# Attention and two expert layers on one core: the queue that issues the transfers of Pool's and VectorE's results

## The chip, the core and the metric

The kernel runs on one core of a Trainium2 chip. The metric is the device time of one execution in microseconds (us), the median of three runs. The engines are TensorE (PE in the profile, its weight loads PEld), VectorE (DVE), ScalarE (ACT), Pool (GpSimd) and SyncE (SP), which here only issues transfers. A transfer is issued by an instruction on an engine's queue and carried out by 16 DMA engines. Transfers that SyncE issues are those of queue q1 in the profile (hardware_dynamic), transfers that Pool issues are those of q0 (software_dynamic).

## What is computed

Three stages follow one another. Only the first is touched by the change. Cut to what matters:

```python
def _attn_ref(q, k, v):                       # (4, 8, 768, 64): batch, heads, positions, width
    block, window = (32, 16); nb = S // block # 24 blocks
    k_sum = k.reshape(B, H, nb, block, D).max(axis=3)
    v_sum = v.reshape(B, H, nb, block, D).mean(axis=3)
    # each position sees its neighbours within 15 places, and the 24 block summaries
    ...
    return np.matmul(a, np.concatenate([v, v_sum], axis=2))
...
x = attn_out.transpose(0, 2, 1, 3).reshape(B * S, H * D)   # 3072 rows of 512
x = _moe_ref(x=x, **moe_kwargs)       # one of 8 experts per row, or none
return _moe2_ref(x=x, **moe2_kwargs)  # 8 experts with 384 rows each, chosen greedily
```

## The kernel before

The attention is `phase_a`. Its work is cut into eight units (a batch and four of its heads), numbered 0 to 7, and each unit into six steps, so that a loop runs over 48 steps and a few more. A step makes four products of queries and keys on TensorE (`qk`, line 128), masks them on VectorE (line 132), takes exponentials on ScalarE, transposes the result, and multiplies it by the values (`pv`, line 154, two steps behind `qk`; the first steps wait until step 4). VectorE divides by the sums (lines 156 to 162). Two units make a batch. After every batch VectorE works out the gate of the first expert layer (`gate1` to `gate3`) and the rows of the batch go to a table in DRAM, `xrows` (line 202), which the first expert layer gathers from.

What a unit needs is loaded by `load`: keys `kt` (line 78) and queries `qd` (line 79) in two halves each, the values once as blocks in `vn` (line 81, the tile is called wraw in the profile), and once in the order in which the products need them, in `VV` (line 85, two transfers into partitions 24 to 119). Partitions 0 to 23 of `VV` take the 24 block means. Those are made by `prep_v`: Pool adds up `vn` in halves (line 118), divides by 32 (line 120), and four transfers, one for each head, copy the 24 rows of means to the twelve places in `VV` (line 122). So a unit's `VV` is complete only when line 85 and line 122 have both landed, and `pv` of the unit's first step waits for that.

`load(u+2)` is written into the second step of unit u. It issues the keys and queries of unit u+2, then calls `prep_v(u+1)`, and then issues the values of unit u+2. For unit 1 the first halving is on VectorE (line 116). The order of the instructions on each engine is the order of the code (the schedule is written by hand), and each queue issues in its order: an instruction that waits holds up everything behind it on its queue. Buffers: `kt` has three, `qd` two, `VV` three, and the raw tiles four. VectorE takes the maxima of the keys in `prep_k` (line 101) and copies them with `prep_kc` (lines 108 and 109).

Of the kernel before, what the change touches and what calls it, by code (L numbers as in the profile page):

```python
# [45 lines left out]
def phase_a(nc,tc,ctx,I,st):  # L46
# [15 lines left out]
    for i in range(2):  # L62
        t=cp.tile([128,2,12,128],F32,name=f"Q2_{i}"); Q2.append(t)
        for h in range(2):
            (G if i else V).memset(t[0:64,h,:,64:128],0.0); G.memset(t[64:128,h,:,0:64],0.0)
    for i in range(3):
        t=cp.tile([24+VP,12,4,65],F32,name=f"VV_{i}")
# [6 lines left out]
    def load(u):  # L74
        b,g=units[u]
        kt=ld.tile([128,2,KW],F32,name="kt",bufs=3); qd=ld.tile([128,2,S],F32,name="qd"); vn=st["raw"].tile([128,2048],F32,name="wraw")[0:96]
        vv=VV[u%3]; src=I['v65']
        def ld_k(h0,h1): nc.sync.dma_start(kt[:,h0:h1],I['k'][b,:,2*g+h0:2*g+h1,:])
        def ld_q(h0,h1): nc.sync.dma_start(qd[:,h0:h1],I['q'][b,:,2*g+h0:2*g+h1,:])
        def ld_v():  # L80
            nc.sync.dma_start(vn,I['v'][b,4*g:4*g+4].rearrange("h (n k) d -> (h n) (k d)",k=32))
        def ld_vv():
            for (s0,s1) in ((0,6),(6,12)):
                ap=bass.AP(tensor=src.tensor,offset=src.offset+(b*2+g)*VR*260+64*260*s0,ap=[[260,VP],[64*260,s1-s0],[1,260]])
                nc.sync.dma_start(vv[24:24+VP,s0:s1].rearrange("p s h d -> p s (h d)"),ap)
        U[u]=dict(kt=kt,qd=qd,vn=vn,vv=vv,q2=Q2[u%2],k2=K2[u%2])
        U[u]['ks']=wk.tile([128,2,24],F32,name="ks",bufs=2)
        ld_k(0,1); ld_q(0,1)
        if u==0: nc.sync.dma_start(cst,I['cst'])
        if u==2: yield; prep_v(1,V)  # L90
        ld_k(1,2); ld_q(1,2)
        if u==0: ld_v(); ld_vv(); nc.sync.dma_start(w17,I['w17'])
        if u==1: prep_v(0,G)
        if u>2: prep_v(u-1,G)
        if u: ld_v(); ld_vv()
        yield
# [16 lines left out]
    def prep_v(u,eng):  # L113
        d=U[u]; vn,vv=d['vn'],d['vv']
        vs2=wk.tile([96,64],F32,name="vs2",bufs=2); w=1024
        if eng is V: V.tensor_reduce(vs2,vn[:,w:2*w].rearrange("p (k d)->p d k",d=64),AX.X,OP.add); w//=2
        while w>=64:
            G.tensor_tensor(vn[:,0:w],vn[:,0:w],vn[:,w:2*w],op=OP.add); w//=2  # L118
        if eng is V: G.tensor_tensor(vn[:,0:64],vn[:,0:64],vs2,op=OP.add)
        G.tensor_scalar(vs2,vn[:,0:64],1.0/32,None,op0=OP.mult)  # L120
        for h in range(4):
            nc.sync.dma_start(vv[0:24,:,h,0:64],vs2[24*h:24*h+24,None,:].to_broadcast([24,12,64]))
    X={}; XT={}; D={}
    def qk(i):
        u,pairs=steps[i]; d=U[u]
# [59 lines left out]
    def group(b,t):  # L185
        return (3,b*NT) if b==B-1 and t==2 else (6,b*NT) if b<B-1 and t==5 else None
# [9 lines left out]
    def gate2(b,t):  # L196
        if group(b,t):
            n,c=group(b,t); c0=c-b*NT; x=X[b][:,c0:c0+n,:]; d,r=D['gd',c]
            s=wk.tile([128,6],F32,name="g_s",bufs=2)[:,0:n]; V.tensor_reduce(s,d,AX.X,OP.add)
            V.tensor_scalar(s,s,1e-9,None,op0=OP.add)  # L200
            V.reciprocal(x[:,:,512],s)
            nc.sync.dma_start(st['xrows'][128+128*c:128+128*(c+n),:].rearrange("(t p) d -> p t d",p=128),x)
            next(r)
    def gate3(b,t):
        if group(b,t): next(D['gd',group(b,t)[1]][1],None)
    def stages(b,t):

        if b<B-2: return tuple(zip(STAGES,(gate1,gate2,gate3,gate3,gate3)))
        if b==B-2: return tuple(zip(STAGES3,(gate1,gate2,gate3,first1,gate3,gate3,first2,first3)))
        return ((1,gate1),(2,gate2),(3,gate3),(4,gate3),(4,gate3))  # L210
# [14 lines left out]
    n=len(steps)  # L225
# [3 lines left out]
    for i in range(n+PL+3):  # L229
        u,t=(i//NT,i%NT)  # L230
# [897 lines left out]
```

## Time and profile before

| | |
|---|---|
| time before, median of 3 runs | 684.64 us (684.58 to 686.84) |
| the profiled execution's own time | 682.42 us |
| its span | 680.8 us |
| busy share of the span: PE, DVE, ACT, POOL | 89%, 75%, 46%, 53% |
| q1 (issued by SyncE): packets, MB | 49968, 79.37 |
| q0 (issued by Pool): packets, MB | 9744, 34.02 |

The span runs from the first to the last instruction of the profiled execution, and its own time is a little more. Busy shares are means over stages with different limits, so a change in one stage has to be read from that stage: the attention takes about the first 176 us. In rows of a timeline the number ahead is the start in us from the beginning of the span, the second the length; in brackets stands how long the engine was idle before, and who ended that.

### The profile page before, as it was taken

The page shows a single profiled execution, that of the slowest core. Times are in us where ns is not written, and L with a number is a line of the kernel's source. Part 1 is how long each engine was busy: PE and PEld are TensorE (multiplying, and loading weights), DVE is VectorE, ACT ScalarE, POOL GpSimd, SP SyncE. Part 2 cuts the span into 40 slices and gives each one's busy share as a digit, 9 for nine tenths or more (in the row PEclk, how much of TensorE's full clock was granted, in tenths as well). Part 3 has the DMA queues.
Part 4 walks back from the last instruction along what each step waited for, and adds up shares of the span by engine and source line. Part 5 has one row for each costly group of instructions (what it writes and reads, how often), then busy time and mean ns, then how long its engine had stood idle before and what let it go on. Part 6 is the DMA issues. An engine that isn't in the chain of part 4 may idle for free.

```text
span 680.8 us, 12765 instructions
## 1 busy us (share of the span) xinstructions
PE 604.4 (89%) x4424; PEld 494.0 (73%) x4427; DVE 508.0 (75%) x1896; ACT 314.2 (46%) x672; POOL 359.0 (53%) x388
## 2 busy tenths in 40 slices
PE   8769896899788999989447999999999999999996
PEld 5658775778466776666226778888797978879895
DVE  5788985999896899994675778788888888862120
ACT  6557774787235676461014235162533426154521
POOL 5234323535462463761016359494876939399841
PEclk9889997999689999898559999999999999999999
DMA  9999999969309968610026063453626254385201
GB/s 258 256 241 249 241 234 206 281 115 339 136 16 324 294 207 287 204 62 23 2 87 208 2 227 115 166 175 124 202 76 203 79 187 155 139 258 180 105 1 46
DMA packets 59778, 114.22 MB, mean 168 GB/s; under 512 B 13537, under 2 KB 23521, under 8 KB 58944
## 3 DMA queue, kind: packets, MB, share of 16 engines
q1 hardware_dynamic: 49968, 79.37, 40.6%
q0 software_dynamic: 9744, 34.02, 15.1%
q8 instruction: 35, 0.57, 0.4%
q14 instruction: 31, 0.25, 0.1%
HBM read 96.54 MB, written 14.88 MB: 164 GB/s over the span
## 4 chain that ended last, share of the span: by engine, by line
PE 18%; issue 11%; POOL 11%; DVE 6%; DMA 3%; ACT 1%; POOLq 1%; DVEq 0%
POOL wl L932 9%; PE dh_ps L961 3%; PE dh_ps L962 3%; PE dh_ps L963 3%; DMA xg<-xrows,p_ix 2%; PE dz_ps L975 2%; PE dz_ps L976 2%; PE dz_ps L977 2%; POOL out_dram L982 2%; DMA wraw<-in_w1b_dram 1%; DVE p_g L793 1%; PE rt_ps L806 1%; PE dx_ps L895 1%; PE dh_ps L950 1%; ACT wh L923 1%
## 5 line engine op out<-in xcount | busy, mean ns | idle before, releaser
L932 POOL TENSOR_TENSOR wl<-wraw,wh 128x512 fp32r<-128x512 f32 x124 | 155.4, 1297 | 5.9 <-ACT wh L923 5.5
L961 PE MATMUL dh_ps<-dxh,wh 128*128 128x384 f32 x256 | 89.2, 349 | 0.7 <-ACT dxh L953 0.7
L923 ACT CAST wh<-wraw 128x512 fp32r<-128x512 f32 x128 | 73.7, 620 | 33.8 <-DMA wraw<-in_w1b_dram 33.4
L962 PE MATMUL dh_ps<-dxl,wh 128*128 128x384 f32 x256 | 86.3, 337 | 0.5 <-DVE dxl L953 0.5
L963 PE MATMUL dh_ps<-dxh,wl 128*128 128x384 f32 x256 | 86.1, 336 | 0.0
L118 POOL TENSOR_TENSOR wraw<-wraw 96x512 f32<-96x512 f32 (+4 forms) x39 | 39.9, 1023 | 80.2 <-DMA wraw<-in_v_dram 77.8
L975 PE MATMUL dz_ps<-wh,dhh 128*128 128x512 f32 x192 | 79.0, 411 | 0.0
L977 PE MATMUL dz_ps<-wh,dhl 128*128 128x512 f32 x192 | 76.0, 396 | 0.0
L976 PE MATMUL dz_ps<-wl,dhh 128*128 128x512 f32 x192 | 75.9, 395 | 0.0
L968 DVE SCALAR_TENSOR_TENSOR dhl<-dh_ps,dhh 128x384 fp32r<-128x384 f32 x64 | 35.1, 554 | 49.0 <-ACT dhh L966 48.7
L982 POOL DMA_INDIRECT out_dram<-dz,io x24 | 24.5, 1023 | 79.5 <-ACT dz L980 76.8
L966 ACT ACTIVATE dhh<-dh_ps 128x384 fp32r<-128x384 f32 x64 | 31.5, 492 | 75.7 <-PE dh_ps L963 74.8
L505 POOL TENSOR_TENSOR wl<-wraw,wh 128x512 fp32r<-128x512 f32 (+1 forms) x26 | 47.8, 1861 | 26.2 <-ACT wh L504 22.7
L980 ACT COPY dz<-dz_ps 128x512 f32<-128x512 f32 x24 | 14.1, 587 | 102.8 <-PE dz_ps L977 56.8
L138 ACT ACTIVATE p_e<-s_sb,nm 128x118 f32<-128x118 f32 x192 | 59.7, 385 | 1.1 <-DVE nm L132 1.1
L128 PE MATMUL s_ps<-kt,Q 128*128 128x118 f32 x192 | 41.4, 299 | 11.6 <-DVE kt L108 9.1
L939 POOL DMA_INDIRECT xg<-xrows,p_ix x24 | 23.3, 972 | 50.9 <-DVE rrow L871 31.3
L961 PEld LDWEIGHTS dh_ps<-dxh,wh 128*128 128x128 f32 x256 | 48.4, 189 | 1.5 <-ACT dxh L953 0.9
L962 PEld LDWEIGHTS dh_ps<-dxl,wh 128*128 128x128 f32 x256 | 48.2, 188 | 1.3 <-DVE dxl L953 1.1
L963 PEld LDWEIGHTS dh_ps<-dxh,wl 128*128 128x128 f32 x256 | 48.1, 188 | 0.0
L504 ACT CAST wh<-wraw 128x1024 fp32r<-128x1024 f32 (+1 forms) x48 | 44.2, 983 | 7.3 <-DMA wraw<-in_w1a_dram 7.1
L132 DVE CUSTOM_DVE_ANT_0 s_sb<-s_ps,cst 128x118 f32<-128x118 f32 x192 | 42.0, 275 | 5.3 <-PE s_ps L128 3.5
(359 smaller groups left out, 1466.5 us busy)
## 6 DMA issues: line engine op xcount, KB each, us to landing
wraw<-in_w1b_dram SPq DMA_DIRECT2D x15, 1024.0 KB
wraw<-in_w2b_dram POOLq DMA_DIRECT2D x14, 1024.0 KB, 7.5
wraw<-in_w2a_dram SPq DMA_DIRECT2D x12, 1024.0 KB
wraw<-in_w1a_dram SPq DMA_DIRECT2D x10, 1024.0 KB
VV<-in_v_dram SPq DMA_DIRECT2D x16, 585.0 KB
kt<-in_k_dram SPq DMA_DIRECT2D x16, 412.0 KB
qd<-in_q_dram SPq DMA_DIRECT2D x16, 384.0 KB
wraw<-in_v_dram SPq DMA_DIRECT2D x8, 768.0 KB
```

The source lines that it names most:

```text
L132: V.tensor_tensor_reduce(out=sb[:,j,:],in0=p[:,j,0:118],in1=mk,scale=-0.125,scalar=3e38,op0=OP.add,op1=OP.min,accum_out=nm[:,j:j+1])
L138: A.activation(pe[:,j,:],sb[:,j,:],AF.Exp,bias=nm[:,j:j+1],scale=-1.0)
L504: (hi.tensor_copy if hi else nc.scalar.copy)(h[:,c],t[:,c])
L505: (lo or nc.vector).tensor_tensor(l[:,c],t[:,c],h[:,c].bitcast(F32),op=OP.subtract)
L923: A.copy(h[:,c],t[:,c])
L932: eng.tensor_tensor(l[:,c],t[:,c],h[:,c].bitcast(F32),op=OP.subtract)
L961: T.matmul(q,wh[:,c],s['xh'][:,d,:],start=(d==0),stop=False)
L962: T.matmul(q,wh[:,c],s['xl'][:,d,:],start=False,stop=False)
L963: T.matmul(q,wl[:,c],s['xh'][:,d,:],start=False,stop=(d==3))
L975: T.matmul(q,s['hh'][:,f,c0],wh[:,c],start=(f==0),stop=False)
L976: T.matmul(q,s['hh'][:,f,c0],wl[:,c],start=False,stop=False)
L977: T.matmul(q,s['hl'][:,f,c0],wh[:,c],start=False,stop=(f==7))
```

## The change

Two lines name another engine for issuing. The four transfers of line 122 and the one of line 202 are issued by Pool in place of SyncE. What they move is the same.

```diff
         G.tensor_scalar(vs2,vn[:,0:64],1.0/32,None,op0=OP.mult)
         for h in range(4):
-            nc.sync.dma_start(vv[0:24,:,h,0:64],vs2[24*h:24*h+24,None,:].to_broadcast([24,12,64]))
+            G.dma_start(vv[0:24,:,h,0:64],vs2[24*h:24*h+24,None,:].to_broadcast([24,12,64]))
...
             V.reciprocal(x[:,:,512],s)
-            nc.sync.dma_start(st['xrows'][128+128*c:128+128*(c+n),:].rearrange("(t p) d -> p t d",p=128),x)
+            G.dma_start(st['xrows'][128+128*c:128+128*(c+n),:].rearrange("(t p) d -> p t d",p=128),x)
             next(r)
```

On SyncE's queue in units 0 and 1 the order changes as follows (kt are keys, qd queries, wraw and VV the values, vs the means).

```order
 L79 DMA qd<-in_q_dram 128x768
-L122 DMA VV_124<-vs_176 24x12x64 x4
 L81 DMA wraw<-in_v_dram 96x2048
 L85 DMA VV_126<-in_v_dram 96x6x260 x2
 L78 DMA kt<-in_k_dram 128x824
 L79 DMA qd<-in_q_dram 128x768
-L122 DMA VV_126<-vs_391 24x12x64 x4
 L78 DMA kt<-in_k_dram 128x824
```

The loads of units 1 and 2 no longer stand behind the means of units 0 and 1.

On the same queue, around unit 4, the piece reads as follows.

```order
-L122 DMA VV_124<-vs_872 24x12x64 x4
 L81 DMA wraw<-in_v_dram 96x2048
 L85 DMA VV_126<-in_v_dram 96x6x260 x2
-L202 DMA xrows<-X_334 128x6x516
 L78 DMA kt<-in_k_dram 128x824
 L79 DMA qd<-in_q_dram 128x768
 L78 DMA kt<-in_k_dram 128x824
 L79 DMA qd<-in_q_dram 128x768
-L122 DMA VV_126<-vs_1174 24x12x64 x4
 L81 DMA wraw<-in_v_dram 96x2048
```

The means of units 3 and 4 and the rows of the first batch have left the queue, and the loads of units 4, 5 and 6 follow each other directly.

On Pool the same transfers have been put in, here behind the sums of unit 3.

```order
 L118 TENSOR_TENSOR wraw<-wraw 96x64
 L120 TENSOR_SCALAR vs_872<-wraw 96x64
+L122 DMA VV_124<-vs_872 24x12x64 x4
 L160 MEMSET X_922 128x6x4
+L202 DMA xrows<-X_334 128x6x516
 L118 TENSOR_TENSOR wraw<-wraw 96x1024
 L118 TENSOR_TENSOR wraw<-wraw 96x512
```

Pool issues the means right behind the multiplication that makes them. The sums of the next unit now stand behind line 202, which waits for VectorE's gate of the first batch.

## Rows read from the trace of the kernel before

**Rows 1.** The page: span, and the share of the DMA engines in 40 slices.

```profile
span 680.8 us, 12765 instructions
...
DMA  9999999969309968610026063453626254385201
```

**Rows 2.** Who waited for whom, VectorE, 0 to 176 us (total, times, longest).

```profile
DVE ks L101 <- DMA kt<-in_k_dram: 11.5, 5, 6.3
```

**Rows 3.** Timeline of VectorE: start, length, what, idle before it and its releaser.

```profile
39.13 0.95 DVE L101 TENSOR_REDUCE ks<-kt 128x24 f32<-128x768 f32 x1 [1.36 <-DMA kt<-in_k_dram]
...
99.13 0.16 DVE L156 TENSOR_SCALAR rs<-o_ps 128x4 f32<-128x4 f32 x1 [0.90 <-PE o_ps L154]
...
103.40 0.23 DVE L181 TENSOR_REDUCE lg<-l_ps 128x17 f32<-128x68 f32 x1 [0.45 <-ACT xT L180]
...
109.96 0.95 DVE L101 TENSOR_REDUCE ks<-kt 128x24 f32<-128x768 f32 x1 [6.34 <-DMA kt<-in_k_dram]
```

**Rows 4.** Windows of 4 us: busy us of each engine, granted clock, DMA share, GB/s.

```profile
20.00:24.00 4.00, 1.68 (x20) 1.50 (x21) 2.99 (x14) 2.31 (x6) 0.00 (x0) 0.89 0.66 152
32.00:36.00 4.00, 3.03 (x40) 2.53 (x40) 3.65 (x21) 2.74 (x10) 0.00 (x0) 1.00 0.63 167
68.00:72.00 4.00, 3.49 (x38) 2.90 (x37) 3.83 (x29) 1.39 (x5) 1.01 (x4) 1.00 0.74 249
72.00:76.00 4.00, 4.00 (x51) 3.29 (x52) 3.90 (x18) 3.59 (x10) 0.00 (x0) 1.00 0.87 202
```

**Rows 5.** Timeline of SyncE's queue: start, length of issuing, line, transfer, count.

```profile
17.76 3.60 SPq L122 DMA_DIRECT2D VV<-vs  x4
...
21.41 0.54 SPq L81 DMA_DIRECT2D wraw<-in_v_dram  x1
...
31.49 3.32 SPq L122 DMA_DIRECT2D VV<-vs  x4
...
85.75 4.40 SPq L122 DMA_DIRECT2D VV<-vs  x4
...
95.29 1.25 SPq L78 DMA_DIRECT2D kt<-in_k_dram  x1
```

**Rows 6.** What SyncE's queue waited for in 0 to 155 us.

```profile
SPq L122 <- POOL X L160: 40.1, 4, 13.9
```

**Rows 7.** Timeline of TensorE: its matmuls of values, units 0 and 1.

```profile
22.22 1.01 PE L154 MATMUL o_ps<-VV,pt_sb 118*64 118x65 f32 x16 [3.68 <-issue]
...
36.55 0.34 PE L154 MATMUL o_ps<-VV,pt_sb 118*64 118x65 f32 x4 [0.53 <-DMA VV<-vs]
```

**Rows 8.** Timeline of Pool: the mean of unit 1, the sums of unit 6, a gather.

```profile
31.10 0.37 POOL L120 TENSOR_SCALAR vs<-wraw 96x64 f32<-96x64 f32 x1
...
121.54 6.13 POOL L118 TENSOR_TENSOR wraw<-wraw 96x1024 f32<-96x1024 f32 x5 [11.96 <-DMA wraw<-in_v_dram]
...
166.48 1.24 POOL L1098 DMA_INDIRECT xg<-xrows,r_gx  x1 [0.88 <-PE pt_ps L143]
```

**Rows 9.** Transfers of Pool's queue: the page's issues; lines 522 and 540.

```profile
wraw<-in_w2b_dram POOLq DMA_DIRECT2D x14, 1024.0 KB, 7.5
...
wraw<-in_w1a_dram POOLq DMA_DIRECT2D x2, 1024.0 KB, 9.9
...
L522 POOL DMA_DIRECT2D wraw<-in_w2b_dram x14: 778/816/857, 358.6 to 600.2; - x14
...
DMA to landing us min/median/max: 3.2/5.6/6.2
```

**Rows 10.** DMA queues (packets, MB, share) in 157:170, 170:176 and 76:110.

```profile
q1 hardware_dynamic: 2284, 4.55, 99.8%
...
q0 software_dynamic: 160, 0.53, 23.2%
...
q1 hardware_dynamic: 5521, 8.15, 107.8%
```

**Rows 11.** Timeline of VectorE: three of the copies of line 108.

```profile
18.64 0.23 DVE L108 COPY kt<-ks 128x144 f32<-128x144 f32 x1
...
43.68 2.37 DVE L108 COPY kt<-ks 128x144 f32<-128x144 f32 x1
...
46.12 1.29 DVE L108 COPY kt<-ks 128x144 f32<-128x144 f32 x1
```

## The prediction

> **What bounds the kernel now.** I read the page first for where the DMA engines are full. They are full or nearly so through the first eight of 40 slices of 17 us, about 136 us, and never again for as long [rows 1]. That is the attention, and no other stage is touched, so I went on with who waits there. VectorE is the engine that hardly rests in it, and its longest waits are for keys: 11.5 us in five waits, one of them 6.3 us [rows 2]. The timeline places the long one. VectorE ends its work of step 28 at 103.6 us and starts the maxima of unit 6's keys at 109.96 [rows 3]. Those keys were issued by SyncE at 95.29 us, behind the means of unit 4, which were issued from 85.75 us on [rows 5]. SyncE's queue in turn was stopped by Pool: the means waited 40.1 us in four waits, the longest 13.9 us [rows 6] (the name is that of the last Pool instruction ahead; what is waited for is the mean of line 120). The windows show what this cost the DMA engines: four stretches of 4 us in which they were busy 0.66, 0.63, 0.74 and 0.87 of the time, so 4 x (0.34 + 0.37 + 0.26 + 0.13) = 4.4 us of idle time before 76 us [rows 4]. Everything else in that stretch is transfers, one behind the other.
>
> **The change part by part.** It removes 32 issues of line 122 and four of line 202 from SyncE's queue, and adds them to Pool.
>
> *SyncE.* Nothing on the queue waits for Pool's means or VectorE's gate any more; what is left are the waits for free buffers and for earlier transfers. The loads then follow each other without the 4.4 us of holes, and unit 6's keys land 4.4 us earlier, at about 105.6 us on the clock of before. They can't come much earlier, since the same bytes have to go ahead of them. Up to 3 us more would be gained if the means and rows no longer go ahead of the keys; that is the length of issuing four means (3.3 us [rows 5]), and I leave it out of the likeliest sum.
>
> *Pool.* An issue of a 1 MB load costs Pool 0.8 us [rows 9], so I take 0.8 us for each of the 36, about 29 us. Pool has the room: ahead of the sums of unit 6 alone it sat idle 12 us, waiting for their load [rows 8]. Behind the issue of line 202 stand the next unit's sums, which now also wait for the gate; those means are needed a unit later. I cost this at nothing; if the cover were gone, 0.8 us for each batch.
>
> *The means' own way.* This is the part that can cost. On SyncE's queue the means of unit 0 were issued from 17.76 us [rows 5] and TensorE, which had nothing else to do and had been idle for 3.7 us, began with them at 22.22 [rows 7]: 4.5 us. Those of unit 1 were issued from 31.49 us [rows 5] and the last head's product began at 36.55 [rows 7]: 5.1 us. SyncE had stopped there, so little lay ahead of them. After the change they go out on Pool's queue while SyncE's is full. No row of before shows a small transfer of Pool beside a full queue of loads, so I bound it. From below: Pool's gathers land in 3.2 us at best [rows 9], which with 0.8 us for each issue gives 0.8 + 3.2 = 4.0 us for the two heads that unit 0's first product needs, and 2.4 + 3.2 = 5.6 us for the four of unit 1, so 0 and 0.5 us late. From nearer by: the longest gather took 6.2 us, and a 1 MB load on Pool's queue takes 9.9 us beside SyncE's loads against 7.5 us [rows 9]. The most telling row is the gather issued at 166.48 us [rows 8], while SyncE's queue kept the DMA engines busy at 99.8%: up to 170 us not one packet of q0 is counted, and after it 160 are [rows 10]. So a full queue does hold up the other one, by some 3.5 us from issue to first packet. I take 6.2 us to land, and 1.5 us more for four transfers that share the engines (half of the 3.3 us that four take alone). Unit 0: 0.8 + 6.2 = 7.0 us against 4.5, 2.5 us late. Unit 1: 2.4 + 6.2 + 1.5 = 10.1 us against 5.1, 5.0 us late, on top of the 2.5, since VectorE's part of unit 1's sums and everything on TensorE stands behind unit 0's product. That is 7.5 us in all. From unit 2 on the means are ready earlier, because their `vn` is loaded earlier, and I count no delay.
>
> *What the delay takes along.* If VectorE comes 7.5 us later to unit 2's keys, its wait of 1.4 us for them is gone [rows 3]. So is the wait of 0.9 us at 99.13 us for a product that stood behind unit 4's means [rows 3]. Two copies of maxima took 2.37 and 1.29 us in place of 0.23 [rows 11], because Pool was adding up unit 2's blocks at the same time; with other timing they may meet or not, and I take half of the 3.2 us, 1.6 us.
>
> *The sum.* Without delay VectorE comes to unit 6's keys at 103.6; with it at 103.6 + 7.5 - 1.4 - 0.9 - 1.6 = 107.2 us. The keys have landed by then (105.6), so it goes on at 107.2 in place of 109.96: 2.8 us gained. Behind that point VectorE is busy without a long wait to the end of the attention, the loads are ahead, and what follows moves along. 682.42 - 2.8 = 679.6 us for the profiled execution. The median of the runs is 2.2 us above that execution, so I predict 684.64 - 2.8 = 681.8, rounded to 682 us.
>
> **The rivals.**
>
> *The queues share well.* The means land as in the bound from below. VectorE would be at unit 6's keys at 103.6 + 0.5 - 3.9 = 100.2 us and wait until they land, at 105.6 us or up to 3 us sooner. The gain is 4.4 to 7.4 us; I take 5.5, which gives 679 us. For it speaks that the loads on Pool's queue lose only 2.4 us beside a full queue [rows 9]; against it that the gather got nothing for 3.5 us. The Trainium skill, "DMA: Bandwidth & Descriptors", section "Queues, rings and completion order", says that a DMA engine goes round the queues that have work and drains a bundle of about 9 to 17 descriptors from one before it goes to the next. By that rule a small transfer would need only a few turns, and this rival would be the case; the rows of the gather don't agree with it at the start of a transfer, and no run here shows the middle of one.
>
> *Turn by turn, and slower.* A unit's means are 4 x 24 x 12 = 1152 small pieces. If each has to let one packet of the loads go first, 1152 packets of SyncE's queue pass meanwhile, and that queue moved 5521 in 34 us [rows 10], so 7.1 us, with their own 3.3 us 10.4 us. Unit 0's first two heads then land 3.5 + 5.2 = 8.7 us after issue (4.2 late), unit 1's 3.5 + 10.4 = 13.9 us (8.8 late). 13.0 - 3.9 is 9.1 us, so VectorE comes at 112.7, 2.7 us later than before; and each later batch boundary, where Pool's sums wait for the gate, can lose a few more, 3 us in all. That is 690 us. It decides from the point where the means of the first two units are more than 10.2 us later together (6.3 us for unit 6's keys and the 3.9 above).
>
> *Nothing moves.* The queue's waits for Pool are replaced at once by waits for buffers that `qk` and `pv` have to free, the holes stay, and the means come neither sooner nor later: 684.6 us. The 4.4 us of holes are against it only if they have no other reason; the waits for Pool are the largest on that queue [rows 6].
>
> **How the numbers follow.** The delayed means, as summed, get 0.40, with a range of their own from 679 to 685 us. The well-shared queue gets 0.33, turn by turn 0.18, nothing 0.09. About 0.5% (3.4 us) is what a measurement of this kernel can tell from no change. Faster by more than that: all of the second and a fifth of the first, 0.41. Slower: the third and a little of the first, 0.20. The rest, 0.39, is within 0.5%. The range of 80% reaches from the middle of the well-shared case with the 3 us that I left out, 677 us, to the end of turn by turn, 690 us.
>
> **What would show it.** SyncE's queue should issue unit 1's values before 17 us in place of 21.41 [rows 5], and have no wait for Pool in the attention; the windows at 20, 32, 68 and 72 us should be full; the 6.3 us wait of VectorE should be gone. The disputed step is read from TensorE: its product of values that stood at 22.22 and 36.55 us should come at about 24.7 and 44, with a wait for the means ahead. If these stand where they did, the second case holds; if unit 1's comes after 47 us, the third. The prediction is wrong in its whole if VectorE waits as long for unit 6's keys as before, or if waits for means appear in units 2 to 7.

## The result and the profile after

The changed kernel takes 690.0 us (median of 20 runs, 687.18 to 701.46). The kernel before takes 686.88 us on the same chip (20 runs, 684.3 to 693.02). The ratio is 1.0054, with a 95% interval of 1.0033 to 1.0074: the change makes the kernel slower by 0.5%, where 682 us and a small gain had been forecast.

The profiled execution after took 689.27 us, close to its median. The one of before, 682.42 us, was 4.5 us under the median of that kernel on this chip. So differences between the two traces up to some 4 us may be chance, and the readings below go by what differs at one place and is repeated in other kernels.

The page shows the DMA engines full up to the eighth slice, as before [rows 1], with a longer span.

```profile
span 687.6 us, 12783 instructions
...
DMA  9999999956506978620026063453626254375201
```

The same four windows as in [rows 4], with the same columns:

```profile
20.00:24.00 4.00, 0.00 (x0) 0.00 (x0) 3.25 (x14) 3.33 (x8) 1.58 (x3) 0.78 1.04 246
32.00:36.00 4.00, 4.00 (x78) 3.69 (x78) 3.04 (x11) 2.82 (x9) 0.00 (x0) 0.94 1.08 377
68.00:72.00 4.00, 4.00 (x53) 3.54 (x50) 3.76 (x14) 3.58 (x11) 3.69 (x4) 1.00 1.04 318
72.00:76.00 4.00, 4.00 (x56) 3.47 (x53) 3.83 (x27) 2.35 (x8) 3.52 (x7) 1.00 1.04 215
```

The holes are closed: the DMA share is 1.04 or more in all four. But in the first of them TensorE does nothing at all. The timeline of SyncE's queue says why the loads are ahead, and that of TensorE (its products of values) what it cost. The heads come in order, and a row of 4 is of one head; unit 0's first step needs two heads, unit 1's four.

```profile
11.90 0.34 SPq L81 DMA_DIRECT2D wraw<-in_v_dram  x1
14.86 2.99 SPq L85 DMA_DIRECT2D VV<-in_v_dram  x2
```

```profile
26.30 0.49 PE L154 MATMUL o_ps<-VV,pt_sb 118*64 118x65 f32 x4 [7.61 <-issue]
28.27 0.92 PE L154 MATMUL o_ps<-VV,pt_sb 118*64 118x65 f32 x12 [1.49 <-DMA VV<-vs]
...
46.26 0.49 PE L154 MATMUL o_ps<-VV,pt_sb 118*64 118x65 f32 x4 [5.82 <-DMA VV<-in_v_dram]
47.09 0.49 PE L154 MATMUL o_ps<-VV,pt_sb 118*64 118x65 f32 x4 [0.34 <-DMA VV<-vs]
48.05 0.70 PE L154 MATMUL o_ps<-VV,pt_sb 118*64 118x65 f32 x8 [0.47 <-DMA VV<-vs]
...
83.40 1.19 PE L154 MATMUL o_ps<-VV,pt_sb 118*64 118x65 f32 x12 [1.30 <-DMA VV<-vs]
86.05 0.34 PE L154 MATMUL o_ps<-VV,pt_sb 118*64 118x65 f32 x4 [1.45 <-DMA VV<-vs]
```

The values of unit 1 are issued at 11.90 us in place of 21.41 [rows 5]. The first products of units 0 and 1 come at 26.30 and 46.26 us. Unit 0's stood at 22.22 [rows 7]; the row of 36.55 there is of unit 1's last head, and its first stood here before:

```profile
34.88 0.52 PE L154 MATMUL o_ps<-VV,pt_sb 118*64 118x65 f32 x8 [0.39 <-DMA VV<-vs]
```

So the first products are 4.1 and 11.4 us late. Unit 0's second head comes at 28.27. The last two heads of unit 1 come from 48.05 us on, so that its last head is at least 11.5 us late. The row of 46.26 names the values as what ended the wait. Unit 1's values were issued by 17.85 us and landed by 33.08; it was the means that were missing, issued from 37.70 us on, the first of them landed at 46.02. Unit 3 waits too, 2.75 us in two pieces. VectorE's waits in 0 to 176 us changed their kind (total, times, longest; two lines of after, then one of before):

```profile
DVE rs L156 <- PE o_ps L154: 13.5, 4, 6.6
DVE ks L101 <- DMA kt<-in_k_dram: 5.3, 3, 3.0
...
DVE rs L156 <- PE o_ps L154: 3.8, 6, 0.9
```

The waits for keys fell from 11.5 to 5.3 us, and the one of 6.3 us [rows 2] is gone. In its place VectorE waits 13.5 us, not 3.8, for TensorE's products, and it comes to unit 6's keys 2.8 us later than before (109.96 [rows 3]):

```profile
112.78 0.95 DVE L101 TENSOR_REDUCE ks<-kt 128x24 f32<-128x768 f32 x1 [0.82 <-DMA kt<-in_k_dram]
```

The second thing that changed is on Pool and, behind it, on VectorE (start, length):

```profile
82.96 0.88 POOL L202 DMA_DIRECT2D xrows<-X  x1 [7.05 <-DVE r_mx L342]
83.86 5.74 POOL L118 TENSOR_TENSOR wraw<-wraw 96x1024 f32<-96x1024 f32 x5
```

```profile
83.15 3.39 DVE L105 COPY K<-kt 128x564 f32<-128x564 f32 x1
86.57 1.52 DVE L112 COPY Q<-qd 64x768 f32<-64x768 f32 x1
89.67 0.45 DVE L105 COPY K<-kt 128x564 f32<-128x564 f32 x1
...
123.93 3.40 DVE L105 COPY K<-kt 128x564 f32<-128x564 f32 x1
127.36 1.51 DVE L112 COPY Q<-qd 64x768 f32<-64x768 f32 x1
```

Pool waits 7.05 us at line 202 for VectorE's gate, issues the rows, and starts unit 4's sums at 83.86, 0.7 us after VectorE has begun its copies behind the gate. The copy that takes 0.45 us at 89.67 takes 3.39 us at 83.15, and 3.40 us at the next batch. Both times it ends 0.3 us after the first of Pool's additions (86.22 and 127.00 us).

How long the means take is read from the DMA view. These are the lines of the means (transfer, queue, count, KB each, median us from issue to landing) for unit 0 (18.1 to 21.6 us, with a load that SyncE issued in the same time), unit 3 (73 to 76 us), and the last unit (150.8 to 153.6 us), when SyncE has nothing under way:

```profile
kt<-in_k_dram SPq DMA_DIRECT2D x1, 412.0 KB, 16.0
...
VV<-vs POOLq DMA_DIRECT2D x4, 72.0 KB, 9.0
...
VV<-vs POOLq DMA_DIRECT2D x4, 72.0 KB, 10.0
...
VV<-vs POOLq DMA_DIRECT2D x4, 72.0 KB, 2.6
```

The same transfers land in 2.6 us beside an empty queue and in 9 to 10 us beside a full one. The queues' lines tell where that time lies (packets, MB, share): unit 0's means from 18.2 to 23.9 us and from 23.9 to 28 us, and the last unit's from 152.1 to 155 us.

```profile
q1 hardware_dynamic: 477, 1.70, 104.4%
...
q1 hardware_dynamic: 464, 0.48, 71.0%
q0 software_dynamic: 189, 0.30, 39.2%
...
q0 software_dynamic: 192, 0.30, 51.2%
```

For 5.7 us after the issue not one packet of Pool's queue is counted. Once they flow, 189 packets pass in 4.1 us beside 464 of SyncE's, against 192 in 2.9 us alone. The delay lies ahead of the first packet, hardly in the sharing.

### The profile page after: what moved, and what is told of

It is laid out like the page before. It is cut to its first block, busy times and chain, and to the rows that moved or that the text cites. A ratio compares the mean times of both kernels' runs of the same rounds, so it can differ in the third digit from the quotient of the medians.

```text
span 687.6 us, 12783 instructions
## 1 busy us (share of the span) xinstructions
PE 607.7 (88%) x4427; PEld 496.9 (72%) x4427; DVE 511.3 (74%) x1896; ACT 313.8 (46%) x672; POOL 386.7 (56%) x424
## 4 chain that ended last, share of the span: by engine, by line
PE 18%; issue 12%; POOL 10%; DVE 6%; DMA 3%; ACT 1%; POOLq 1%; DVEq 0%
POOL wl L932 8%; PE dh_ps L961 3%; PE dh_ps L962 3%; PE dh_ps L963 3%; DMA xg<-xrows,p_ix 2%; PE dz_ps L975 2%; PE dz_ps L976 2%; PE dz_ps L977 2%; POOL out_dram L982 2%; DMA wraw<-in_w1b_dram 1%; DVE p_g L793 1%; PE rt_ps L806 1%; PE dx_ps L895 1%; PE dh_ps L950 1%; PE rt_ps L802 0%
## 5 line engine op out<-in xcount | busy, mean ns | idle before, releaser
L923 ACT CAST wh<-wraw 128x512 fp32r<-128x512 f32 x128 | 73.7, 619 | 35.7 <-DMA wraw<-in_w1b_dram 34.3
L154 PE MATMUL o_ps<-VV,pt_sb 118*64 118x65 f32 x768 | 37.6, 241 | 20.3 <-issue 7.6
L154 PEld LDWEIGHTS o_ps<-VV,pt_sb 118*64 118x64 f32 x768 | 29.6, 148 | 30.6 <-issue 13.8
L963 PEld LDWEIGHTS dh_ps<-dxh,wl 128*128 128x128 f32 x256 | 48.7, 190 | 0.0
L145 ACT COPY pt_sb<-pt_ps 118x512 f32<-118x512 f32 x48 | 28.0, 584 | 43.4 <-PE pt_ps L143 43.4
```

Of the source, the lines that this page charges most:

```text
L154: T.matmul(o[r:r+64,k,0:65],pts[:,j,64*e:64*e+64],d['vv'][0:118,w,2*h+e,:],start=True,stop=True)
L923: A.copy(h[:,c],t[:,c])
L963: T.matmul(q,wl[:,c],s['xh'][:,d,:],start=False,stop=(d==3))
```

## The experiments

The ratios are to the kernel before on the same chip, each with its 95% interval. Their half widths are 0.2 to 0.4% for most, which is what can't be told from no change. In some of these kernels the line numbers are one to five higher than in the changed one.

**Each half alone.** First the means on Pool with the rows on SyncE:

```diff
-            G.dma_start(st['xrows'][128+128*c:128+128*(c+n),:].rearrange("(t p) d -> p t d",p=128),x)
+            nc.sync.dma_start(st['xrows'][128+128*c:128+128*(c+n),:].rearrange("(t p) d -> p t d",p=128),x)
```

> Only line 122 is on Pool, line 202 is back on SyncE's queue. Theory A (the loss is that the means of units 0 and 1 land late on Pool's queue, beside a full queue of loads): TensorE's first products of units 0 and 1 stand as late as with the whole change, near 26 and 46 us, and the time stays within 2 us of the whole change, 0.3 to 0.8% above before. Theory B (the loss is that Pool stops at line 202 until VectorE's gate and then runs its sums against VectorE's copies): the copies of line 105 that took 3.4 us near 83 and 124 us are short again, and the time falls by 3 us or more, to that of before.

Measured: 688.7 us, ratio 1.0033 [1.0004, 1.0063]. TensorE's products:

```profile
27.37 0.48 PE L154 MATMUL o_ps<-VV,pt_sb 118*64 118x65 f32 x4 [8.16 <-issue]
...
47.26 0.49 PE L154 MATMUL o_ps<-VV,pt_sb 118*64 118x65 f32 x4 [6.03 <-DMA VV<-vs]
```

They are as late as with the whole change, the profile names the means this time, and no copy behind a gate is long. Then the rows on Pool with the means on SyncE:

```diff
-            G.dma_start(vv[0:24,:,h,0:64],vs2[24*h:24*h+24,None,:].to_broadcast([24,12,64]))
+            nc.sync.dma_start(vv[0:24,:,h,0:64],vs2[24*h:24*h+24,None,:].to_broadcast([24,12,64]))
```

> Only line 202 is on Pool, line 122 is back on SyncE's queue. Theory A: the products of units 0 and 1 begin at 22 and 35 us as before, and the time is that of before within 2 us, or up to 3 us less, since the loads no longer wait behind the gate. Theory B: the two copies near 80 and 122 us take 3 us or more, and the time is 3 us or more above before.

Measured: 685.39 us, ratio 0.9982 [0.9948, 1.0015]: no change that can be told. The products (unit 0's first, unit 1's last) stand at 22.51 and 37.79 us. The copies behind the gates take 1.65 and 3.51 us. So the means alone make the kernel slower, by 0.3%, barely clear of noise. Whether the whole change (1.0054) loses more than that, these two don't tell: the intervals overlap.

**The early means back on SyncE.**

```diff
+            (nc.sync if u<2 else G).dma_start(vv[0:24,:,h,0:64],vs2[24*h:24*h+24,None,:].to_broadcast([24,12,64]))
```

> The change with the means of units 0 and 1 back on SyncE's queue, those of units 2 to 7 and the rows on Pool. Theory A: the 8.3 us that units 0 and 1 lost are back, of which up to 5 us go to waits for unit 6's keys or to later units; 682 to 686 us where before has 686 to 687. Theory B: the same copies collide, and the time stays within 2 us of the whole change.

Measured: 691.88 us, ratio 1.0077 [1.0039, 1.0114]. My theory missed, and the time is theory B's, within 2 us of the whole change; the copies behind the gates take 3.40 and 3.39 us. The first products of units 0 and 1 are early again (24.56 and 37.38 us), but now those of unit 2 wait:

```profile
62.12 0.34 PE L154 MATMUL o_ps<-VV,pt_sb 118*64 118x65 f32 x4 [1.54 <-issue]
64.58 0.49 PE L154 MATMUL o_ps<-VV,pt_sb 118*64 118x65 f32 x4 [2.12 <-DMA VV<-vs]
66.31 0.48 PE L154 MATMUL o_ps<-VV,pt_sb 118*64 118x65 f32 x4 [1.24 <-DMA VV<-vs]
```

Their means were issued at 52.67 us and the unit had begun at 50.5. In the changed kernel they were issued at 49.10 us and the unit, put off by units 0 and 1, began at 57.3. The lateness belongs to no unit. A unit's first product stands three steps behind its first mask in the code (`LAGS`; not two), and the wait shows where that slack is too short: in the changed kernel in unit 3, which begins 2.5 us after the issue of its means, and not in unit 2, which begins 8.2 us after.

**SyncE held back until the means are made.**

```diff
+        nc.sync.dma_start(hold,vs2[0:1,0:1])
```

> The change with one transfer of 4 bytes added on SyncE's queue behind each unit's means, which waits for the mean of line 120 and holds up SyncE's queue where line 122 held it before. The means still go out on Pool. Theory A in its form that the full queue of loads is what delays Pool's transfers: with the queue held, the means of units 0 and 1 land within 5 us of issue, and TensorE's products begin at 22 to 24 us and 36 to 39 us. Rival to it (Pool's queue is slow for these small pieces whatever SyncE does): they begin near 26 to 28 and 46 to 48 us as with the whole change.

Measured: 691.52 us, ratio 1.0074 [1.0041, 1.0106]. It tells little: SyncE was let go at 18.08 us and issued its next loads from 18.86 us on, while Pool was still issuing its four transfers (18.37 to 21.29 us). They landed 8.5 us after issue, and the first product came at 25.72.

**SyncE held back until the means have landed (units 0 and 1).**

```diff
+        if u<2: nc.sync.dma_start(hold,vv[0:1,0,:,0:1])
```

> The changed kernel, with a transfer of 4 bytes on SyncE's queue behind the means of units 0 and 1 that waits until these means have landed, so that SyncE adds nothing to its queue in between, as it stood before the change. Theory A (what delays a transfer of Pool's queue is what SyncE has issued and still issues beside it): the first products of values come near where they stood before, 22 to 24.5 us and 36 to 39 us; the long waits of TensorE for the means in units 0 and 1 (7.6 and 5.8 us in the changed kernel) fall to 4 us or less; the time goes to 686 to 690 us, since the holes in the loads are back. Rival (Pool's queue is slow to start and to carry these pieces, whatever SyncE does): the products stay at 26 to 28 and 46 to 48 us, and the time gets worse than the changed kernel's, 691 to 695 us, because the loads then wait for late means as well.

Measured: 694.23 us, ratio 1.0085 [1.0047, 1.0123]. The transfers of Pool's queue in units 0 and 1, then TensorE's products:

```profile
VV<-vs POOLq DMA_DIRECT2D x4, 72.0 KB, 4.3
...
VV<-vs POOLq DMA_DIRECT2D x4, 72.0 KB, 4.7
```

```profile
23.11 0.49 PE L155 MATMUL o_ps<-VV,pt_sb 118*64 118x65 f32 x4 [4.19 <-issue]
...
41.07 1.13 PE L155 MATMUL o_ps<-VV,pt_sb 118*64 118x65 f32 x16 [3.80 <-DMA VV<-vs]
```

The same queue, the same pieces: 4.3 and 4.7 us from issue to landing in place of 9.0 and 8.5. From issue to first product it is 4.3 us (18.81 to 23.11) and 5.5 us (35.54 to 41.07), where SyncE's own queue needed 4.5 us and 3.4 us (31.49 to 34.88) before [rows 5, 7]. So it is mainly SyncE's traffic that delays the means, not Pool's queue. The products came near the places forecast for this theory (unit 1's by 2 us later), but the time is the rival's: the holes are back, and longer, since SyncE now waits to 25.11 and 41.76 us for the landing.

**Another second queue.** ScalarE issues the means, a step after they are made; the rows are on SyncE.

```diff
+        def send():
+            for h in range(4):
+                A.dma_start(vv[0:24,:,h,0:64],vs2[24*h:24*h+24,None,:].to_broadcast([24,12,64]))
+        D['send',u]=send
...
+        if i in SEND: D.pop(('send',SEND[i]))()
```

> The means are issued from ScalarE's queue, a step after they are made, the rows of line 202 from SyncE's: to be held beside the kernel with only the means on Pool's queue (688.7 us). Theory A (any second queue stands behind what SyncE has issued): the first product of unit 0 again at 26 us or later and that of unit 1 at 44 us or later, and a median of 687 to 692 us. Rival (it is Pool's own queue, whose transfers are made by software, that is slow): the first products within 2 us of those before, at 22 to 24.5 and 36 to 39 us, the wait for the keys of unit 6 short, and a median of 679 to 684 us.

Measured: 712.42 us, ratio 1.0355 [1.0321, 1.0389]. Unit 0's first product comes at 27.00 us, 7.8 us after the issue at 19.18, but TensorE shows no wait for means there. It had stood 6.67 us, until 24.05, for ScalarE's exponentials. SyncE had stopped too, 7.1 us at line 81 until the first of these means had landed (22.98 us), so unit 0 tells nothing of a full queue. Unit 1 does. Its means are issued from 35.70 us on. The queues' lines from 35.7 to 41 us, where no packet of ScalarE's queue (q10) is counted, and from 41 to 44 us (packets, MB, share):

```profile
q1 hardware_dynamic: 523, 1.49, 104.1%
...
q10 hardware_dynamic: 315, 0.08, 16.9%
```

That is 5.3 us without a packet, so the delay is not special to Pool's queue. The loss beyond it is a new one, in ScalarE's timeline, its waits, and the lengths of its issues (in ns, min/median/max):

```profile
35.70 8.91 ACTq L123 DMA_DIRECT2D VV<-vs  x4
...
57.92 12.41 ACTq L123 DMA_DIRECT2D VV<-vs  x3
70.38 0.58 ACT L147 COPY pt_sb<-pt_ps 118x512 f32<-118x512 f32 x1 [12.57 <-DMA VV<-vs]
...
ACT pt_sb L147 <- DMA VV<-vs: 24.5, 4, 12.6
...
L123 ACTq DMA_DIRECT2D VV<-vs x32: 789/790/1407, 19.2 to 175.7; - x32
```

An issue takes 0.79 us. The rows of 8.91 and 12.41 us are mostly a wait ahead of the last issue. In unit 2 that issue, at 69.55 us, waits on the semaphore that the first head's means, issued at 57.06, use as well, and these land at 69.53. ScalarE's copies for TensorE stand behind. Pool's four issues never took more than 3.25 us in the changed kernel.

**The rows behind the next sums.** Pool issues line 202 of the first two batches after the next unit's sums and means, with the means on SyncE (first) and on Pool (second).

```diff
+        if 'rows' in D: D.pop('rows')()
...
+            f=lambda: G.dma_start(st['xrows'][128+128*c:128+128*(c+n),:].rearrange("(t p) d -> p t d",p=128),x)
+            if b<2: D['rows']=f
+            else: f()
```

> The means are back on SyncE's queue; the rows of the first two batches are issued by Pool behind the next unit's sums, not ahead of them. To be held beside the kernel with only the rows on Pool (685.4 us). Theory B (line 202 holds Pool's sums until the gate and so puts them beside VectorE's copies behind it): the two copies of line 105 behind the gates take at most 1.5 us each in place of 1.65 and 3.5, and the median is 1 to 4 us lower, 681.5 to 684.5 us. Rival (the copies meet Pool's sums wherever these stand, or what is saved there is lost as a wait further on): copies over 2 us elsewhere, and a median within 1 us of 685.4.

> The whole change, with the rows of the first two batches behind the next unit's sums. To be held beside the changed kernel (690.0 us). Theory B: the two copies behind the gates, 3.4 us each in the changed kernel, fall under 1.5 us, and the median falls by 2 to 5 us to 685 to 688 us, about that of the kernel with only the means on Pool (688.7) or a little below. Rival (the copies cost nothing in the end): the copies are short and the median stays within 1 us of 690. The late products of units 0 and 1 stay at 26 to 28 and 45 to 48 us under both.

Measured, first: 685.13 us, ratio 0.9968 [0.9938, 0.9998], against 0.9982 with the rows ahead. The copies of line 105 at the gates take 1.62 us and less, but there is one of 1.61 elsewhere, and two of line 108 of 2.41 and 1.30. The rival holds here. Second: 687.61 us, ratio 0.9986 [0.9954, 1.0017], against 1.0054 [1.0033, 1.0074] for the change as made. The intervals don't meet. VectorE behind the two gates:

```profile
88.17 0.44 DVE L105 COPY K<-kt 128x564 f32<-128x564 f32 x1
...
124.07 0.45 DVE L105 COPY K<-kt 128x564 f32<-128x564 f32 x1
```

The two copies save 2 x 2.95 = 5.9 us on VectorE. The medians differ by 2.4 us (690.0 and 687.61); the ratios, each to the kernel before as measured beside it, differ by 0.7% (0.3 to 1.1%), some 5 us. With late means, then, where line 202 stands on Pool is worth about that; with the means in time it was worth nothing that can be told. Why it differs stays open. And the first products are as late here as with the whole change (27.91 and 46.42 us), yet the time is that of before. With the rows behind the sums, late means cost 0.2% (0.9986 against 0.9968), which can't be told from nothing.

**Pool for later units alone.** Rows behind the sums, as above, and the means of units 3 to 7 (first) or 4 to 7 (second) on Pool:

```diff
+            (nc.sync if u<3 else G).dma_start(vv[0:24,:,h,0:64],vs2[24*h:24*h+24,None,:].to_broadcast([24,12,64]))
```

> The means of units 0 to 2 are issued by SyncE as before, those of units 3 to 7 by Pool; the rows of the first two batches by Pool behind the next unit's sums. Theory (the change loses where means are late in units 0 and 1 and where Pool's sums meet the copies behind the gate, and gains where unit 6's keys come sooner): products of units 0 to 2 where they stood before, unit 3's up to 3 us late, the wait of VectorE for unit 6's keys under 2 us, and a median of 681 to 685 us, 2 to 5 us under that of before. Rival (as when units 0 and 1 alone went back: whichever unit's means come first behind a full queue is late by as much): unit 3's first product 5 us late or more, and a median of 686 to 691 us.

> As the kernel with the means of units 3 to 7 on Pool's queue, but those of unit 3 on SyncE's too. The means of unit 4 are the ones that stood in front of unit 6's keys. Theory: no first product later than before by more than 2 us, the wait for unit 6's keys still under 3 us, and a median of 681 to 685 us. Rival (the lateness moves to unit 4): unit 4's first product behind a wait of 3 us or more, and a median of 686 to 690 us.

Measured, first: 695.82 us, ratio 1.0114 [1.0059, 1.0169]. Again the first unit whose means Pool sends is late; they are issued at 72.57 us and the product comes 11.2 us later:

```profile
83.73 0.70 PE L155 MATMUL o_ps<-VV,pt_sb 118*64 118x65 f32 x8 [4.93 <-DMA VV<-vs]
```

The rival's sign; the time lies above both ranges. Second: 688.71 us, ratio 0.9997 [0.9954, 1.0039]. No product waits more than 1.4 us for means, the longest wait for keys is 2.8 us, and the time is that of before all the same, in the rival's range without its sign. In unit 6 VectorE waited 2.20 us for rows that were still being sent, so I took the rows off Pool again. Against the kernel before:

```diff
-            nc.sync.dma_start(vv[0:24,:,h,0:64],vs2[24*h:24*h+24,None,:].to_broadcast([24,12,64]))
+            (nc.sync if u<4 else G).dma_start(vv[0:24,:,h,0:64],vs2[24*h:24*h+24,None,:].to_broadcast([24,12,64]))
```

> Only the means of units 4 to 7 go on Pool's queue, those of units 0 to 3 and all rows stay on SyncE's. To be held beside the kernel with the same means and the rows on Pool behind the next unit's sums, which won 2.6 us up to the start of unit 6 and lost them in it, on longer copies and on a wait of 2.2 us for rows still being sent. Theory (what is left of the gain is eaten by the rows on Pool): no long wait for unit 6's keys, no wait of VectorE for rows, no late means, and a median of 682 to 685 us, 2 to 5 us under that of before. Rival (the long wait for keys was no more than slack of one execution, and the loads don't set the end): a median within 2 us of that of before, 685.5 to 689 us, with waits of the same sum in other places.

Measured: 685.57 us, ratio 0.9995 [0.9967, 1.0024]. The rival's time again.

**The means on SyncE, but behind the values** (from unit 2 on), with the rows behind the sums on Pool:

```diff
+        if u<2: send()
+        else: D['send']=send
...
         if u: ld_v(); ld_vv()
+        if 'send' in D: D.pop('send')()
```

> All means on SyncE's queue, but from unit 2 on issued behind the values of the next unit, not ahead of them; the rows of the first two batches by Pool behind the next unit's sums. Theory (the holes in the loads come from what stands behind the waiting means, and a mean that waits where SyncE would soon wait for a buffer anyway costs nothing): the values of units 4 and 5 are issued 5 us or more sooner, the keys' wait of VectorE in unit 6 goes down from 6.3 to 3 us or less, and the median is 681 to 685 us. Rival (the means then stand behind 1.3 MB more of loads and come late, or the holes only move to the next keys): waits of TensorE for the means of 3 us and more in units 2 to 7, or a wait for unit 6's keys as long as before, and a median of 686 to 691 us.

Measured: 687.38 us, ratio 1.0014 [0.9978, 1.005]. Unit 2's means are made at 53.2 us, issued behind the values from 56.80 us on, and the issuing alone takes 8.89 us; a product of that unit waits 8.91 us. The rival's case.

**No means at all, from unit 3 or 4 on.** What is left of the gain if nothing is sent?

```diff
+            if u<3: nc.sync.dma_start(vv[0:24,:,h,0:64],vs2[24*h:24*h+24,None,:].to_broadcast([24,12,64]))
```

> As before, but the transfers of the means of units 3 to 7 are left out (the products then use older means of the same buffer), so SyncE waits for no mean from unit 3 on and no mean can be late: a bound on what any other place for them could bring. The later layers see other values, so the attention is read by itself as well. Theory C (the holes in the loads set the end of the attention): the long wait for unit 6's keys is gone, the first step of unit 6 is masked 4 us or more before 132.6 us, and the median is 678 to 683 us. Rival D (the loads have slack or meet other limits, and the long wait for keys is paid back elsewhere): the first step of unit 6 within 2 us of 132.6 us, and a median of 685 to 688 us.

> The same with the transfers of units 4 to 7 left out alone: the bound for the kernels that sent those of units 4 to 7 through Pool's queue, which came to the time of before. Theory C: a median of 680 to 684 us, and unit 6 begun 3 us or more before 132.6 us. Rival D: 685 to 688 us, and unit 6 begun within 2 us of 132.6 us.

Measured: 877.0 and 717.85 us. These times tell nothing of the attention, since the expert layers behind it got other rows; the attention is read from the timeline of VectorE, at the first mask (line 132) of units 2, 4 and 6 and of the last step.

| kernel | unit 2 | unit 4 | unit 6 | last step |
|---|---|---|---|---|
| before | 49.0 | 88.8 | 132.6 | 162.9 |
| the change | 57.3 | 95.9 | 136.7 | 168.5 |
| Pool from unit 4, rows behind | 48.7 | 91.7 | 130.0 | 162.6 |
| Pool from unit 4, rows on SyncE | 49.5 | 92.0 | 132.4 | 164.4 |
| no means from unit 3 | 46.7 | 90.1 | 130.6 | 160.8 |
| no means from unit 4 | 47.2 | 90.2 | 129.6 | 160.7 |

Unit 6 begins 2.0 and 3.0 us sooner than before, and the last step 2.1 and 2.2 us sooner. That is, in one execution of each, the most that any other place for these means could bring; at unit 6 it is less than the 4 us of theory C for the first kernel, and its bound for the second. But unit 2 already begins 2.3 and 1.8 us sooner, and up to there these programs are the same as before. What is gained from there on, by leaving the means out, is -0.2 and 0.4 us at the last step, which one execution of each can't tell from nothing. VectorE in the first of the two kernels, total and times of its waits for keys, and the longest:

```profile
DVE ks L101 <- DMA kt<-in_k_dram: 11.3, 5, 5.4
...
54.04 0.95 DVE L101 TENSOR_REDUCE ks<-kt 128x24 f32<-128x768 f32 x1 [5.42 <-DMA kt<-in_k_dram]
```

The waits for keys add up to 11.3 us, as before (11.5 [rows 2]), though no mean holds SyncE from unit 3 on. The long one has moved from unit 6's keys to unit 3's, which VectorE takes at the start of unit 2. Up to that point the program is the same as before.

## Why the prediction was wrong

**Right: what happens on SyncE's queue.** The holes are filled, unit 1's values go out 9.5 us sooner, no wait of that queue for Pool's means is left (the one that the view still puts down to Pool, 4.3 us at line 263, is of a transfer of zeros), and the long wait for unit 6's keys is gone, as "What would show it" listed.

**Right in kind, too small: the means' own way.** "I take 6.2 us to land": it was 9.0 for unit 0. The 7.0 us that it summed for unit 0's first two heads were 10.1 (18.21 to 28.27), so "2.5 us late" was 5.6. Unit 1's own term was about right: 10.1 us forecast, at least 10.35 from issue to last head (37.70 to 48.05). But its means were issued 6.2 us later than before (37.70 and 31.49), and the 7.5 us in all were 11.5 or more. That is past the 44 us at which the product was expected, and past the 47 us and the 10.2 us that it had named as signs of the third case. With 11.5 in place of 7.5 its own sum has VectorE at unit 6's keys at 103.6 + 11.5 - 3.9 = 111.2 us, a loss of 1.2; it was 112.78. The third rival's 690 us was the time that came, but by luck, for the way it gave was another. The row of the gather [rows 8, 10] had shown 3.5 us without a packet, and I took the landing time of another gather over it. It was 5.7 us here. The middle of the way was the milder part: that rival's turn by turn took each of 1152 pieces for a packet, and Pool's queue sends 192 packets for a unit. The rule on bundles in the Trainium skill, "DMA: Bandwidth & Descriptors", section "Queues, rings and completion order", agrees with the trace once the packets flow (189 in 4.1 us beside 464 of SyncE's), and not for the 5.7 us ahead of them; the well-shared case that it would have given did not come.

**Wrong: "From unit 2 on the means are ready earlier ... and I count no delay."** Unit 3 waited 2.75 us, which the prediction had listed among the signs of being wrong in its whole, and in the runs with Pool from unit 2 or 3 on the first such unit waits too, up to 4.93 us at a time. The sums did not get far enough ahead of their units for the 9 to 11 us that the means then take.

**Wrong: "I cost this at nothing"** (Pool's sums behind line 202). The copies of line 108, on which 1.6 us were taken as saved, were indeed short (0.35 us at most), but the wait set Pool's sums beside VectorE's copies of line 105 at two batch boundaries, 2 x 2.95 us on VectorE and 0.7% by the ratios of the kernels with and without that wait. I asked who waits for Pool's sums, and not whom they slow down when they start at another time.

**Wrong: the sum as a whole.** It took the wait of 6.3 us in one execution as the gain to be had, 4.4 us of it by closing holes. With those means not sent at all the attention ended 2.1 us sooner, a lead that was there at unit 2. That the waits for keys kept their sum and moved to unit 3's keys speaks for the 6.3 us being one place at which a general lag of the loads came to light, not the price of the means in front. Against a gain of at most some 2 us stand the late means (0.33% or 2.3 us alone) and the collisions. The two don't simply add up, since the late means cost nothing that can be told once the collisions at the gates were gone. The rest of the account is open: why the kernels with Pool from unit 2 or 3 on were no better than the whole change (ratios 1.0077 and 1.0114, with intervals that overlap its own), though fewer units were late, the traces do not settle.

No kernel here beats that of before by more than 0.5%. The best is 0.9968, with the rows alone on Pool behind the next sums, barely apart from 1.

## What to carry to other kernels

A small transfer that someone waits for is not freed by giving it a queue of its own: beside a full queue of loads it starts only some 6 us after its issue, so it needs a slack of about 10 us here, or must stand where the loads pause, as on SyncE's queue before. When an instruction that waits is put on an engine, ask also what the work behind it will then run beside. And a long wait in one profiled execution is no gain to be had until a run in which its cause is left out shows the end of the stage to move, counted from where the two programs begin to differ.

## What the runs showed of the hardware beyond that

Pool's queue sends the same means in fewer packets: 51714 in the whole execution with the means alone on Pool, against 59778 when SyncE or ScalarE issues them. Issues on ScalarE's queue took 0.79 us each, but the engine stood up to 12.6 us ahead of a copy until a transfer of its own had landed. Pool's issues took 0.66 us in the median and 0.97 at most. And a copy of VectorE that starts while Pool issues line 202, with a long addition behind, took 3.39 to 3.51 us in place of 0.44 in the five kernels where the two met so behind a gate.
